# Two float32 attention groups ahead of the MLP, and a pair of token tiles as the MLP's first block

## The chip, the cores and the metric

The kernel runs on one core of a Trainium2 chip. The metric is the device time of one execution in microseconds (us); the trace is of one profiled execution, and its times count from the first instruction. TensorE is called PE, VectorE DVE, ScalarE ACT, GpSimd POOL, and SP is the engine whose queue issues all of this kernel's DMAs. PEld is PE's weight load.

## The reference

Forgetting attention (4 batches, 8 heads, 576 positions, 64 dims), then two MLPs over 2304 tokens:

```python
scores = scale * q @ k.T                      # per head, causal
cum = cumsum(log(clip(f, 1e-4, 1.0)))
scores = where(causal, -1e9, scores + cum[:, None] - cum[None, :])
attn = softmax(scores) @ v
x = attn, heads side by side                  # 2304 x 512
x = leaky(x @ w_in, 0.01) @ w_out             # 512 -> 2048 -> 512
out = leaky(x @ moe2_w_in, alpha) @ moe2_w_out
```

## The kernel before

**Work and tiles.** Tokens are taken in eight *head groups*: each batch is cut into its first 320 positions and its last 256 (`ORDER`: four groups of the first kind, then four of the second). A group of the first kind treats its 8 heads as 4 pairs; a pair has two full units of 128 queries for each head (against 128 and 256 keys) and one packed unit, in which both heads' 64 last queries share 128 rows (against 320 keys). The first MLP goes over token tiles of 256. A *block* is one tile or, where `PAIRS` names it, a pair of tiles; before, the blocks are tiles 0, 1 and 2 alone and the pairs (3,4), (5,6), (7,8). In a block of one tile each matmul streams 256 columns, in a pair 512. Per block there are 16 slices `f` of the hidden dimension, each with 12 matmuls for the hidden values (`moe_h`, L588) and 12 for the output (`moe1_y`, L641). The second MLP follows on its own (L752, L821).

**Number formats.** Most operands are split into a high and a low part in a reduced float32 form (fp32r), with three products. The first `NAT = 16` heads, groups 0 and 1, are computed in plain float32 instead ("native"): each score or value matmul is then two instructions. Before, q and k of a native head stand twice, on partitions 0 to 63 and 64 to 127, and the scale is halved for it (`-SCALE / 2`).

**Weights.** They arrive as float64 bit patterns. Each of the 32 halves of the first MLP's weights is loaded (`raw`, 512 KB), put together by one ACT and three DVE operations (`assemble`, L477, L484, L487, L492) and split into high and low (L395, L400). 18 of the halves are written to `wscr` and loaded again for each later block; 14 stay in SBUF. All this is due in the first block, since that block uses every half once.

**Order.** Nothing is ordered by hand. `Plan.run` plays the program through with a duration for each operation (`t_mm`, `t_act`, ...) and a due time, and what it takes first on a free engine is issued first; every engine and SP's queue then run in that fixed order. `PROL` and `FIRST0` say when the first block is due to begin and how long it lasts.

**Start.** `fg` is loaded, its logarithm summed by a scan (`cum`), and two rows per head are stored to `cum_d` and loaded again for each head, spread over partitions (`cb`, L908). For head 0 alone PE does that spreading (L932). A unit is then: scores (L1095) with a mask matmul (L1100), the decay and the row maximum on DVE (L1109), `exp` on ACT (L1120), 1e-9 and a reciprocal on DVE (L966, L969), the scaling (L1135 or L1137), transposes on PE (L1150), their eviction (`pt`), the value matmuls (L988 native, L998 else) and the split into the MLP's input (`xp`). Group 0 is meant for the prologue; group 1 is planned into block 0, group 2 into block 1, and so on: a block needs the groups that hold its tokens.

**Leaky in the first MLP.** `small` takes 0.01 h from PSUM to `gr` (ACT, L598, or DVE, L600), `leaky1` takes the maximum of both on DVE (L603); then `gr` is split into `g` (hi, lo).

Of the kernel before, what the change touches and what calls it, by code (L numbers as in the profile page):

```python
# [19 lines left out]
P = 128  # L20
# [3 lines left out]
SUBD = 1  # L24
MARGIN = 450
# [11 lines left out]
NY = 2  # L37
TAGS = ("bx bx bx b1 b1 b0 b0", "by by by by bx bx bx", "b0 b0 b1 b1 by by by")
# [14 lines left out]
PAIRS = (3, 5, 7)  # L53
SHIFT = 1
PROL = 26500
FIRST0 = 54400
# [204 lines left out]
def t_mm(n, passes=1):  # L261
    return passes * max(n / 2.4 + 2.5, 109)
# [43 lines left out]
def tile_forgetting_attention_two_moe(ctx: ExitStack, tc, qk0, qk1, v0, v1, fg, w1, w2, alphaT, out):  # L306
# [18 lines left out]
    STREAM = [HALVES[1 + i * (len(HALVES) - 4) // (NSTREAM - 1)] for i in range(NSTREAM)]  # L325
# [61 lines left out]
    pools, rings, att_rings = {"sb": sb, "conv": conv}, {}, []  # L387
# [16 lines left out]
    def ring(tag, bufs, shape, dtype=F32, pool="sb", after=None):  # L404
        def make(slot):
            name = f"{tag}_{slot}"
            return pools[pool].tile(shape, dtype, tag=name, name=name, bufs=1)

        rings[tag] = Ring(bufs, make, after)
        if pool == "att":  # L410
            att_rings.append(rings[tag])
# [15 lines left out]
    xp = [sb.tile([P, 2, NC, 2 * T], F32R, name=f"xp{i}") for i in range(2)]  # L427
    for i in range(4):
        rings[f"x{i}"] = Ring(1, lambda slot, i=i: xp[i // 2][:, :, :, i % 2 * T :][:, :, :, :T])
# [15 lines left out]
    ring("tri", 1, [P, 2 * P], F32R, pool="att")  # L445
# [69 lines left out]
    def weight1(f, half, d):  # L515
        v = assemble(0, f, half, d)
# [53 lines left out]
    def moe_h(bi, f0, hp=None):  # L570
# [5 lines left out]
        xs = [x_tile(k) for k in BLOCKS[bi]]  # L576

# [6 lines left out]
        def mm(i, w, c0, c1):  # L584
            def fn():
                for c in range(c0, c1):
                    for k, (a, s) in enumerate(((0, 0), (0, 1), (1, 0))):
                        pe.matmul(  # L588
                            h()[:, i] if single else h(), lhsT=w.ap[:, a, c * P : (c + 1) * P],
                            rhs=xs[0].ap[:, s, c] if single else xp[(BLOCKS[bi][0] + SHIFT) % 4 // 2][:, s, c],  # L590
# [5 lines left out]
        def small(e):  # L596
            if e == "act":
                act.activation(out=r(), in_=h(), func=AF.Copy, scale=0.01)  # L598
            else:
                dve.tensor_scalar(out=r(), in0=h(), scalar1=0.01, scalar2=None, op0=ALU.mult)  # L600

        def leaky1():
            dve.tensor_tensor(out=r(), in0=h(), in1=r(), op=ALU.max)  # L603
# [16 lines left out]
        plan.op(t_cast(n, True), u, small, r=[hp], w=[gr])  # L620
        on("dve", t_dve(n), u, leaky1, r=[hp], w=[gr])
# [50 lines left out]
    def moe2_x(bi):  # L672
# [3 lines left out]
        for k, tag in enumerate(tags):  # L676
            if tag in ("b0", "b1"):
# [5 lines left out]
                views.append(lambda i=i, at=at: xp[i].rearrange("p a b c -> p (a b c)")[:, at : at + 4 * N2].rearrange(  # L683
# [177 lines left out]
    def attention_heads(gi, hs, d, span):  # L861
# [6 lines left out]
        pt, nm, pair = new("pt"), new("nm"), None  # L868
# [22 lines left out]
        for e, h in enumerate(hs):  # L891
            r, dh = b * H + h, d + each * e
            even = h % 2 == 0
            qk, cb = new("qk"), new("cb")
# [4 lines left out]
            if even:  # L899
                vr = x_raw["v"] = new("vr")  # L900
                on("dma", t_dma(3 * nkt * D * 4 * P), dh - 12e3, lambda: sp.dma_start(
                    out=vr.ap[:, :nkt], in_=g["v"][b, h // 2]), w=[vr])

            def load_qk(qk=qk, h=h):
                sp.dma_start(out=qk.ap[:, : n + keys], in_=g["qk"][b, h])
# [20 lines left out]
            on("dma", t_dma((n + keys) * 4 * P), dh - 7e3, load_qk, w=[qk])  # L926
            if gi == 0 and h < NBC:
# [3 lines left out]
                def broadcast(r=r, bp=bp, m=m):  # L931
                    pe.matmul(  # L932
                        bp.ap[:, :m], lhsT=f32(tri_b.ap[: B * H, r : r + 1]).to_broadcast([B * H, P]),
                        rhs=origin_b[0].ap[: B * H, :m], start=True, stop=True,
# [3 lines left out]
                plan.op(t_cast(m, True), -6e3, lambda en, cb=cb, bp=bp, m=m: cast(en, cb.ap[:, :m], bp.ap[:, :m]), r=[bp], w=[(cb, 0)])  # L938
            else:
                on("dma", t_dma(m * 4 * P), dh - 6.5e3, lambda r=r, cb=cb, m=m: load_cum(lambda: cb.ap[:, :m], r, m), r=[cum_b], w=[(cb, 0)])  # L940
            if pack:
# [3 lines left out]
                on("dma", t_dma(keys * 4 * D), dh - 6e3, lambda r=r, half=half: load_cum(  # L945
                    lambda: pair.ap[half, S - keys :], r, keys), r=[cum_b], w=[(pair, 1 + e)])
            if not native:
                plan.op(t_cast(n + keys), dh - 2e3, qk_hi, r=[qk], w=[k1], shared=True)
# [4 lines left out]
            q, ks = (qk, [qk]) if native else (k1, [k2, k1])  # L953
            for u in full:
                i = len(todo)
                du = d + span * i / count
                todo.append((i, u, attention_scores(g, u, i, du, [(q, ks)], cb, 0, nm, native), [e], du))
            work.append((h, q, ks, v2, o2, even, lo, hi))
        if pack:
            i, u = len(todo), g["units"][-1]  # L960
            du = d + span * i / count
            todo.append((i, u, attention_scores(g, u, i, du, [w[1:3] for w in work], pair, S - keys, nm, native), [0, 1], du))
        for i, u, t, es, du in todo:

            def guard(i=i):
                dve.tensor_scalar(out=nm.ap[:, 3, i : i + 1], in0=nm.ap[:, 2, i : i + 1], scalar1=1e-9, scalar2=None, op0=ALU.add)  # L966

            def recip(i=i):
                dve.reciprocal(out=nm.ap[:, 3, i : i + 1], in_=nm.ap[:, 3, i : i + 1])  # L969

            on("dve", 70, du, guard, w=[(nm, i)])
            on("dve", 75, du, recip, w=[(nm, i)])
            attention_weights(g, u, i, du, t, es, nm, pt, pt_pair if len(es) > 1 else pt_ap, native)
        for e, (h, _, _, v2, o2, even, lo, hi) in enumerate(work):
# [78 lines left out]
    def attention_scores(g, unit, u, d, heads, cb, cb0, nm, native):  # L1053
# [4 lines left out]
        t, dm = new("t"), None if native or pack else new("dm")  # L1058
# [17 lines left out]
        else:  # L1076
            on("pool", t_pool1(nk - split) - 100, d - 1e3, mask, r=[cb], w=[dm])
# [3 lines left out]
        for i, (lo, hi, dec, d0) in enumerate(parts):  # L1081
            if sp_ is None or nk > 512:
                s0, s1 = (0, nk) if nk <= 512 else (lo, hi)
                sp_ = new("a")
                for e, (q, ks) in enumerate(heads):

                    def scores(sp_=sp_, s0=s0, s1=s1, e=e, q=q, ks=ks):
# [280 lines left out]
```

## Time and profile before

| | |
|---|---|
| time, median of 3 runs (lowest, highest) | 1003.78 us (1002.88, 1005.05) |
| profiled execution, first to last instruction | 1001.4 us |
| PE busy | 976.0 us (97%) |
| DVE, ACT, POOL busy | 789.9, 545.3, 94.1 us |
| granted TensorE clock, mean | 0.995 |
| DMA moved | 213.5 MB |

The profiled execution's span and the median of the timed runs differ by 2.4 us; what lies around the span is in that difference. PE's matmuls are pipelined, and the end of one is modelled: a matmul's "mean ns" holds its latency, so the cost of one in a dense stretch is read from the distance between starts.

### The profile page before, as it was taken

Reading aid. Unit: us, or ns where it says so; the run is one execution under the profiler, and the core shown is the slowest. Engines: PE = TensorE matmul, PEld = TensorE weight load, DVE = VectorE, ACT = ScalarE, POOL = GpSimd, SP = SyncE. Lnnn points to the kernel's source line nnn. Section 1 sums busy time; section 2 is a strip of 40 time slices with the busy share of each in tenths; the row PEclk is TensorE's granted clock in tenths of the full one; section 3 lists DMA queues with packets and bytes.
Section 4 is the critical chain, followed back from the end, with each engine's and each line's share of the span. In section 5 each row is a group of like instructions: output and inputs, shape, how many; then the busy total and the mean of one; then the engine's idle time right before and its main releaser. Section 6 shows DMA issues by size and latency. Waiting matters only on the chain.

```text
span 1001.4 us, 16762 instructions
## 1 busy us (share of the span) xinstructions
PE 976.0 (97%) x5538; PEld 866.5 (87%) x5538; DVE 789.9 (79%) x2024; ACT 545.3 (54%) x1239; POOL 94.1 (9%) x169
## 2 busy tenths in 40 slices
PE   5999899999999999999999999999999999999998
PEld 3788799999988888888888888989898898988987
DVE  7889977889999998998788768965686656856563
ACT  6877777788887887887765436311242112321112
POOL 1100111122122212221110000000000000000000
PEclk9999999999999999999999999999999999999999
DMA  8999987788887867987288764543364433544311
GB/s 267 302 316 344 337 268 253 243 293 280 298 299 234 270 214 237 307 275 233 80 288 328 266 209 137 192 143 104 120 206 143 142 103 122 181 136 140 103 52 64
DMA packets 80199, 213.51 MB, mean 213 GB/s; under 512 B 8720, under 2 KB 25520, under 8 KB 80112
## 3 DMA queue, kind: packets, MB, share of 16 engines
q1 hardware_dynamic: 80112, 212.44, 64.0%
q8 instruction: 44, 0.72, 0.3%
q14 instruction: 43, 0.35, 0.1%
HBM read 178.73 MB, written 33.67 MB: 212 GB/s over the span
## 4 chain that ended last, share of the span: by engine, by line
PE 83%; DVE 6%; issue 4%; DMA 4%; ACT 2%; POOL 0%; SPq 0%; ACTq 0%; POOLq 0%; DVEq 0%
PE bank L821 20%; PE bank L752 18%; PE bank L641 16%; PE bank L588 15%; PE bank L1095 5%; PE bank L998 4%; PE bank L1150 4%; DMA w2in<-wa 1%; PE bank L988 1%; DMA vr<-v 1%; DVE pt L1166 1%; DMA raw<-w 1%; DVE t L1109 1%; DMA cb<-cum_d 1%; DVE g L400 0%
## 5 line engine op out<-in xcount | busy, mean ns | idle before, releaser
L821 PE MATMUL bank<-w,g 128*128 128x512 f32 x756 | 196.9, 393 | 0.0
L395 ACT ACTIVATE g<-r 128x384 fp32r<-128x384 f32 x96 | 50.4, 525 | 253.5 <-DVE r L784 232.0
L761 DVE TENSOR_TENSOR r<-bank,r 128x384 f32<-128x384 f32 x168 | 91.1, 554 | 89.8 <-PE bank L752 89.4
L821 PEld LDWEIGHTS bank<-w,g 128*128 128x128 f32 x756 | 140.1, 188 | 21.2
L641 PE MATMUL bank<-g,ws 128*128 128x256 f32 (+1 forms) x720 | 145.5, 343 | 0.3 <-ACT g L395 0.2
L641 PEld LDWEIGHTS bank<-g,ws 128*128 128x128 f32 x720 | 113.3, 191 | 14.0 <-ACT g L395 1.2
L588 PE MATMUL bank<-xp,w 128*128 128x256 f32 (+1 forms) x576 | 115.4, 341 | 0.4 <-ACT pt L395 0.4
L588 PE MATMUL bank<-xp,ws 128*128 128x256 f32 (+1 forms) x576 | 115.4, 341 | 0.0
L588 PEld LDWEIGHTS bank<-xp,w 128*128 128x128 f32 x576 | 90.2, 189 | 12.5 <-ACT pt L395 0.6
L588 PEld LDWEIGHTS bank<-xp,ws 128*128 128x128 f32 x576 | 89.8, 190 | 10.1 <-issue 0.5
L1120 ACT ACTIVATE t<-t,nm 128x128 f32<-128x128 f32 (+4 forms) x144 | 83.4, 580 | 16.3 <-DVE nm L1109 15.4
L641 PE MATMUL bank<-g,w 128*128 128x256 f32 (+1 forms) x432 | 87.9, 342 | 0.0
L1135 ACT ACTIVATE t<-t,nm 128x128 f32<-128x128 f32 (+4 forms) x123 | 70.8, 583 | 21.1 <-DVE nm L969 18.1
L1150 PE MATMUL bank<-tri,t 128*128 128x128 f32 x432 | 72.3, 279 | 7.8 <-DVE gr L603 3.1
L395 ACT ACTIVATE pt<-bank 128x512 fp32r<-128x512 f32 (+6 forms) x174 | 70.0, 425 | 14.8 <-PE bank L1150 13.8
L641 PEld LDWEIGHTS bank<-g,w 128*128 128x128 f32 x432 | 66.9, 190 | 7.8 <-ACT xp L395 0.5
L400 DVE TENSOR_TENSOR g<-r,g 128x384 fp32r<-128x384 f32 x96 | 53.1, 554 | 26.0 <-ACT g L395 25.8
L1061 POOL TENSOR_SCALAR_AFFINE_SELECT dm<-cb 128x448 f32<-128x448 f32 (+1 forms) x96 | 50.1, 524 | 227.3 <-DVE nm L1109 186.8
L1166 DVE TENSOR_TENSOR pt<-bank,pt 128x128 fp32r<-128x128 f32 (+2 forms) x136 | 65.5, 503 | 4.9 <-ACT pt L395 4.1
L1150 PEld LDWEIGHTS bank<-tri,t 128*128 128x128 f32 x432 | 50.8, 142 | 17.7 <-ACT t L1135 5.6
L603 DVE TENSOR_TENSOR gr<-bank,gr 128x512 f32<-128x512 f32 x72 | 49.3, 685 | 13.5 <-ACT gr L598 12.7
L998 PEld LDWEIGHTS bank<-pt,v 128*128 128x128 f32 x416 | 54.9, 188 | 5.1 <-DVE pt L1166 1.1
(138 smaller groups left out, 1753.9 us busy)
## 6 DMA issues: line engine op xcount, KB each, us to landing
ws<-wscr SPq DMA_DIRECT2D x90, 512.0 KB, 4.9
raw<-w SPq DMA_DIRECT2D x64, 512.0 KB, 5.7
wa<-w2in SPq DMA_DIRECT2D x33, 512.0 KB, 3.5
ws<-w2in SPq DMA_DIRECT2D x33, 512.0 KB, 3.4
qk<-qk SPq DMA_DIRECT2D x32, 416.0 KB, 4.4
qk<-qk SPq DMA_DIRECT2D x32, 320.0 KB, 5.0
wscr<-ws SPq DMA_DIRECT2D x18, 512.0 KB, 5.5
cb<-cum_d SPq DMA_DIRECT2D x32, 288.0 KB, 4.4
```

The costliest lines, as they stand in the source:

```text
L395: act.activation(out=out, in_=in_, func=AF.Copy)
L400: (dve if e == "dve" else gps).tensor_tensor(out=out, in0=in0, in1=in1, op=ALU.subtract)
L588: pe.matmul(h()[:, i] if single else h(), lhsT=w.ap[:, a, c * P : (c + 1) * P], rhs=xs[0].ap[:, s, c] if single else xp[(BLOCKS[bi][0] + S ...
L641: pe.matmul(out(c), lhsT=w.ap[:, a, col : col + P], rhs=g.ap[:, s, at : at + n], start=f == 0 and (a, s) == (0, 0) and (c % 2 == 0 or not ...
L752: pe.matmul(b.ap[:, :N2], lhsT=t.ap[:, a, o + c * P : o + (c + 1) * P], rhs=view(k)[:, s, c], start=c == 0 and i == 0, stop=c == 1 and i == 2,
L761: on("dve", t_dve(N2), d + k * step - URGENT, lambda: dve.tensor_tensor(out=out.ap, in0=b.ap[:, :N2], in1=x.ap, op=ALU.add), r=[b] if x is ...
L821: pe.matmul(acc[j * (N2 // P) + t].ap, lhsT=g.ap[:, s, t * P : (t + 1) * P], rhs=w.ap[:, a], start=p == 0 and i == j and (a, s) == (0, 0), ...
L998: pe.matmul(po.ap[:, q:n], lhsT=v2.ap[:, o2 + j, :], rhs=pt_ap(s, e, j, j + 1, q, n), start=s == 0 and j == 0, stop=s == 1 and j == nkt - 1,)
L1120: act.activation(out=t.ap[:, :nk], in_=t.ap[:, :nk], func=AF.Exp, scale=-1.0, bias=nm.ap[:, last, u : u + 1], accum_out=nm.ap[:, 2, u : u ...
L1135: act.activation(out=t.ap[:, :nk], in_=t.ap[:, :nk], func=AF.Copy, scale=nm.ap[:, 3, u : u + 1])
L1150: pe.transpose(tp.ap[:, (j - j0) * P : (j - j0 + 1) * P], t.ap[:, k0 : k0 + P], f32(tri_b.ap[:, :P]))
L1166: dve.tensor_tensor(out=lo, in0=src, in1=f32(hi), op=ALU.subtract)
```

## The change

1. `PAIRS` gets a 0: tiles 0 and 1 become one block, so the blocks are (0,1), 2, (3,4), (5,6), (7,8). `xp` is laid out tile by tile, so a pair's right-hand operand is two runs of 256 columns instead of one of 512.
2. Groups 0 and 1, the native ones, are both planned ahead of the first block, in a pool of their own (`att0`) with deeper rings: 12 score tiles, 3 `qk0`, 3 `cb0`, 3 `vr0`, 2 `pt0`, 4 `nm0`. When all their operations are done, the pool is closed and `att` opened in its place; no operation of a later group starts before. The due times become `PROL = 52000`, `FIRST0 = 99000`.
3. A native head's q and k are loaded once, to 64 partitions: the even head to 0..63, the odd head to 64..127 of one tile. The score matmuls contract over 64 rows, and the scale is whole.
4. The leaky function of the first MLP becomes one ACT operation, `AF.Prelu` with `alpha=0.01`, from PSUM.
5. 1e-9 and the reciprocal are taken for two units at once (`RECIPS = 2`).
6. The planner prices matmuls at `n / 2.4 + 13` ns.
7. The loads of `cum_d` wait for their own group kind's store, not for both; the first 8 weight halves (`FREE`) stay in SBUF and the 18 that are streamed come after them; weight loads from the second slice on wait for the stores of `cum`. The tiles of the prologue's scan lie in the MLP's rings, `tri` in the main pool.

```diff
+RECIPS = 2
...
+NQ0 = 3
+NV0 = 3
+NB0 = 3
+NT0 = 12
...
-PAIRS = (3, 5, 7)
+PAIRS = (0, 3, 5, 7)
...
-PROL = 26500
-FIRST0 = 54400
+PROL = 52000
+PROL0 = 26000
+FIRST0 = 99000
+FREE = 8
...
-    return passes * max(n / 2.4 + 2.5, 109)
+    return passes * max(n / 2.4 + 13, 113)
...
-    STREAM = [HALVES[1 + i * (len(HALVES) - 4) // (NSTREAM - 1)] for i in range(NSTREAM)]
+    STREAM = [HALVES[FREE + i * (len(HALVES) - 3 - FREE) // (NSTREAM - 1)] for i in range(NSTREAM)]
...
-    xp = [sb.tile([P, 2, NC, 2 * T], F32R, name=f"xp{i}") for i in range(2)]
+    xp = sb.tile([P, 4, 2, NC, T], F32R, name="xp")
...
+    ring("qk0", NQ0, [P, 640], pool="att0")
+    ring("vr0", NV0, [P, 3, 3, D], pool="att0")
+    ring("cb0", NB0, [P, 832], pool="att0")
+    ring("t0", NT0, [P, 320], pool="att0")
+    ring("nm0", 4, [P, 4, 5], pool="att0")
+    ring("pt0", 2, [P, 1408], pool="att0")
...
-                            rhs=xs[0].ap[:, s, c] if single else xp[(BLOCKS[bi][0] + SHIFT) % 4 // 2][:, s, c],
+                            rhs=xs[0].ap[:, s, c] if single else xp[:, x0 : x0 + 2, s, c],
...
-        def leaky1():
-            dve.tensor_tensor(out=r(), in0=h(), in1=r(), op=ALU.max)
+        def leaky():
+            act.activation(out=r(), in_=h(), func=AF.Prelu, alpha=0.01)
...
-        plan.op(t_cast(n, True), u, small, r=[hp], w=[gr])
-        on("dve", t_dve(n), u, leaky1, r=[hp], w=[gr])
+        on("act", t_act(n) - 40, u, leaky, r=[hp], w=[gr])
...
-                sp.dma_start(out=qk.ap[:, : n + keys], in_=g["qk"][b, h])
+            def load_qk(qk=qk, h=h, rows=rows):
+                sp.dma_start(out=qk.ap[rows, : n + keys], in_=g["qk"][b, h, : rows.stop - rows.start])
...
-                                sp_.ap[:m, : s1 - s0], lhsT=q.ap[:, qe - m : qe], rhs=k.ap[:, o : o + s1 - s0], start=j == 0,
+                                sp_.ap[:m, : s1 - s0], lhsT=q.ap[rows, qe - m : qe], rhs=k.ap[rows, o : o + s1 - s0], start=j == 0,
...
-                    scale=-SCALE / 2 if native else -SCALE,
+                    scale=-SCALE,
...
+            if i % RECIPS == 0:
+                i1 = min(i + RECIPS, len(todo))
...
-    attention(0, 0.0, PROLOGUE)
+    attention(0, 0.0, PROL0)
+    attention(1, PROL0, PROLOGUE - PROL0)
+    natives = [o for o in plan.ops if any(b.ring in att_rings["att0"] for b in o.bufs)]
+    opened = on(None, 0, 0.0, reopen(nctx, "att", "left", actx), after=natives)
+    for k in att_rings["att"]:
+        k.after = opened
...
-            weight1(f, half, due(0, f) - W1LEAD + 1e3 * half)
-    sent = 1
+            weight1(f, half, due(0, f) - W1LEAD + 1e3 * half, stored if f else [])
+    sent = 2
```

## Rows read from the trace of the kernel before

**Rows 1.** Stretches: length, busy PE, PEld, DVE, ACT, POOL (count), clock, DMA share, GB/s.

```profile
0.00:18.00 18.00, 11.10 (x29) 7.19 (x29) 11.28 (x29) 10.50 (x23) 1.75 (x12) 1.00 0.79 263
18.00:28.30 10.30, 6.43 (x20) 4.58 (x21) 9.10 (x41) 8.25 (x26) 2.13 (x6) 0.67 0.87 275
28.30:75.00 46.70, 44.32 (x295) 37.74 (x294) 38.26 (x136) 36.67 (x113) 4.36 (x8) 1.00 0.94 312
75.00:125.00 50.00, 43.17 (x301) 38.73 (x300) 48.74 (x127) 37.83 (x90) 4.50 (x7) 0.97 0.96 341
...
135.10:201.40 66.30, 66.30 (x557) 66.24 (x556) 54.05 (x196) 51.18 (x147) 11.34 (x29) 1.00 0.77 249
...
300.00:450.00 150.00, 148.86 (x837) 126.94 (x837) 142.24 (x386) 122.55 (x261) 33.99 (x49) 1.00 0.80 257
...
0.00:201.40 201.40, 181.25 (x1271) 163.82 (x1272) 168.76 (x550) 152.82 (x418) 25.74 (x65) 0.97 0.87 291
```

**Rows 2.** SP's queue in order of time: the stores that end blocks 0 and 1.

```profile
135.09 0.90 SPq L662 DMA_DIRECT2D yd<-ysb  x2
...
201.42 0.89 SPq L662 DMA_DIRECT2D yd<-ysb  x2
```

**Rows 3.** The chain that ended last, 0 to 130 us: start, length, what.

```profile
13.82 5.36 DMA cb<-cum_d
...
36.82 6.32 DMA raw<-w
```

**Rows 4.** Line L487 alone, once per weight half: DVE busy, clock, DMA share, GB/s.

```profile
62.00:135.10 73.10, 14.34 (x21) 0.98 0.95 327
```

**Rows 5.** PE in order of time: start, length, line; the bracket is the idle before.

```profile
21.87 0.77 PE L1095 MATMUL bank<-qk 128*128 128x128 f32 x2 [4.16 <-DVE nm L1109]
...
27.96 2.43 PE L988 MATMUL bank<-pt,vr 128*128 128x320 f32 x12
30.23 1.47 PE L1150 MATMUL bank<-tri,t 128*128 128x128 f32 x9
31.54 0.60 PE L1095 MATMUL bank<-qk 128*128 128x256 f32 x2
...
32.03 0.44 PE L1095 MATMUL bank<-qk 128*128 128x128 f32 x2
...
32.36 0.65 PE L1095 MATMUL bank<-qk 128*128 128x256 f32 x2
...
32.91 2.33 PE L988 MATMUL bank<-pt,vr 128*128 128x320 f32 x12
35.08 0.60 PE L1150 MATMUL bank<-tri,t 128*128 128x128 f32 x4
35.61 0.75 PE L1095 MATMUL bank<-qk 128*64 128x320 f32 x2
36.30 0.97 PE L588 MATMUL bank<-xp,w 128*128 128x256 f32 x6
...
51.85 2.38 PE L988 MATMUL bank<-pt,vr 128*128 128x320 f32 x12
```

**Rows 6.** The chain again, dense stretches of a single block and of a pair.

```profile
62.44 1.43 PE bank L588 x12
...
542.61 2.72 PE bank L588 x12
```

**Rows 7.** Groups by line and form: count, busy us, mean ns, idle before.

```profile
L598 ACT ACTIVATE gr<-bank 128x512 f32<-128x512 f32 x68 | 40.4, 594 | 33.4 <-PE bank L588 32.5
...
L1239 ACT ACT_TABLE_LOAD x1 | 1.3, 1283 | 0.0
...
L603 DVE TENSOR_TENSOR gr<-bank,gr 128x512 f32<-128x512 f32 x72 | 49.3, 685 | 13.5 <-ACT gr L598 12.7
...
L969 DVE RECIPROCAL nm<-nm 128x1 f32<-128x1 f32 x144 | 22.1, 158 | 1.4
...
L600 DVE TENSOR_SCALAR gr<-bank 128x512 f32<-128x512 f32 x4 | 2.7, 684 | 0.2 <-PE bank L588 0.2
```

## What the change was predicted to do

> **What bounds the kernel now.** I read the stretches first. From 135 us to 626 us PE is busy practically without a gap, of which one stretch stands for all: 66.30 of 66.30 us between 135.10 and 201.40, at full clock, with DVE at 54 and ACT at 51 [rows 1]. There the kernel is bound by PE, and only fewer or cheaper matmuls help. Before 125 us it is not: PE has gaps in each of the four stretches, and between 75 and 125 us DVE is busy 48.74 of 50 us [rows 1]. So the question is what the first blocks cost beyond their PE work. The second view, SP's queue, gives their ends: block 0 ends at 135.1 us, block 1 at 201.4 us [rows 2]. The third, PE in order of time, prices the work in dense stretches by the distance between starts. A native pair: nine transposes 30.23 to 31.54 = 1.31 us; a unit of 256 keys with its mask 31.54 to 32.03 = 0.49; one of 128 keys 32.03 to 32.36 = 0.33; one half of the packed unit 35.61 to 36.30 = 0.69; the value matmuls 32.91 to 35.08 = 2.17 [rows 5]. Together 1.31 + 2 x (0.49 + 0.33) + 2 x 0.69 + 2.17 = 6.50 us, for the 8 pairs 52.0 us. Twelve matmuls of 256 columns take 1.43 us, of 512 columns 2.72 us, that is 119.2 and 226.7 ns each [rows 6].
>
> So up to 201.4 us PE had 52.0 us of native work, 2 x 384 matmuls x 119.2 ns = 91.5 us of MLP, and 66.3 - 45.8 = 20.5 us of other attention (what block 1's stretch holds beside its 384 matmuls). The sum is 164.0 us; 37.4 us were lost. The fourth view, the chain, says to what. First the start: it passes through a load of `cb` at 13.82 for 5.36 us [rows 3], PE resumes at 21.87 [rows 5], and the clock is 0.67 between 18 and 28.3 us [rows 1]. Then the weights: at 36.82 the chain goes through a load of `raw` of 6.32 us [rows 3], and 21 of the 32 halves are put together only between 62 and 135 us [rows 4], while block 0 has a mere 45.8 us of matmuls to cover that work. That is where DVE is full and PE waits.
>
> **The change, part by part.** *Both native groups first.* PE has no MLP work to fill with until the second group is through, so the end of the native part, T, is the main term. The start is not changed in kind: `cb` of all heads but one still comes through `cum_d`. That its loads wait for one store rather than two saves at most what lies between two issues; I count nothing. PE resumes at 21.9 us. By then it can have done the first pair's scores (6.50 - 1.31 - 2.17 = 3.0 us) and, of head 0 and the next pair, some 1.1 us more: 4.1 us, an estimate; 47.9 us remain. The clock of 0.67 over 10.3 us is 6.8 us at 1.2 instead of 2.4 GHz, in which PE was busy 6.43 us [rows 1]: half of it, 3.2 us, is lost again. For gaps I take what the stretch from 28.3 to 75 us shows, 46.70 - 44.32 = 2.4 us [rows 1]; bounds are nothing and the slow pace among the rivals. T = 21.9 + 47.9 + 3.2 + 2.4 = 75.4 us.
>
> *The pair as first block.* 384 matmuls of 226.7 ns are 87.0 us instead of 91.5, a gain of 4.5 us. Its first matmuls wait for the last eviction and split, an estimate of 1.0 us from the ACT and DVE operations of [rows 7], which are larger. The other attention again takes 20.5 us. The same work is then done at 75.4 + 1.0 + 87.0 + 20.5 = 183.9 us instead of 201.4: 17.5 us gained.
>
> This holds if DVE and ACT keep up. To 201.4 us they were busy 168.8 and 152.8 us [rows 1]. Of DVE's share 16 x 0.685 = 11.0 us of L603 go, and by the reciprocals taken in pairs 24 of 60 units' two small operations, 24 x 2 x 0.158 = 7.6 us (the addition taken at the reciprocal's price) [rows 7]. That leaves 150.2 us in 183.9, 82%, and ACT 83%. The 32 halves now have from the start to the end of an 87 us block rather than of a 46 us one. So PE sets the pace in the pair, and I count nothing for their wait; if the halves came late again, it would cost part of what was lost between 75 and 125 us, 6.8 us of idle PE [rows 1].
>
> *q and k once.* The same number of loads, half the bytes, the same columns in PE: nothing. It is hidden by the native work itself; its price if the clock or the pace suffers stands under the rivals. *Two runs of 256 columns* in the pair's operand: not below nothing, since the columns stay; not over the price of a second matmul start, 2 x 119.2 - 226.7 = 11.7 ns for 4 x 192 = 768 matmuls, 9.0 us. What a matmul costs beyond its columns is about the same at 256 and at 512 (119.2 - 106.7 = 12.5 and 226.7 - 213.3 = 13.4 ns), so it goes by the instruction; I take nothing.
>
> *Leaky on ACT.* 68 of the 72 first steps were on ACT already (594 ns); the second step, 72 x 685 ns = 49.3 us of DVE [rows 7], goes. Where PE is full that buys nothing. Between 300 and 450 us DVE is busy 142.24 of 150 us and PE idles 1.14 us [rows 1]; I take 0.9 of it. ACT needs 594 ns for this shape and DVE 684 [rows 7]. The Trainium skill (ScalarE: Activation LUTs, Rules for kernel authors) advises the opposite for functions like relu and max, VectorE rather than ScalarE; for this float32 tile in PSUM the two rows disagree with it, and by the rule the 0.9 us would be lost, the sum 986.3 us.
>
> *Reciprocals in pairs* make a unit wait for the exponential of its neighbour, with DVE's queue behind it. Twelve score tiles cover that in the native part, the MLP's matmuls later. Without the cover it is one ACT operation, about 0.6 us [rows 7], for each of 24 native batches, 14 us: the slow pace below. *The pool* that opens only after the native part delays the third group's loads to T; 87 us of MLP matmuls cover them. *The planner's price of a matmul* (12 ns more) changes orders; I count nothing and leave it in the range.
>
> The sum: 17.5 + 0.9 = 18.4 us. The profiled span of 1001.4 becomes 983.0 us; the median of the runs lies 2.4 us above the span, so the prediction is 985.4 us.
>
> **The rivals.** *A slow native part* (chance 0.17). PE is alone with chains of scores, DVE, ACT, transposes and evictions, and has nothing to fill gaps. Before, the first group's value matmuls came at 27.96 to 51.85 us, three steps of 7.96 us [rows 5] instead of 6.50, though a weight load and some MLP work were in it. At that pace T is 27.96 + 7 x 7.96 + 2.2 = 85.9 us, 10.5 us later: 995.9 us.
>
> *The clock, the other side* (0.09). The native scores now use 64 of the array's rows, and a stretch of nothing but native work could be held at 1.2 GHz. For it: between 18 and 28.3 us, scores, masks and transposes alone kept PE busy 6.43 us, and the clock stood low for 6.8 us. Against it: from 28.3 to 75 us, mostly native work, it was full [rows 1]. All of it at the low level gives T = 21.9 + 95.8 + 2.4 = 120.1 us and a time of 1030 us. It decides from (18.4 - 2.0) x 2, about 33 us at 1.2 GHz: less than that is still a gain.
>
> *The split operand costs its 11.7 ns* (0.07): 994.4 us.
>
> *Two heads side by side* (0.05). The packed unit's two halves now lie on different rows of the array; if they ran at once, 8 x 0.69 = 5.5 us would go, and the time would be 979.9 us. Masks stand between the other scores. No row shows it, since all of before use 128 rows. The Trainium skill (TensorE: Matmul & The Clock Gate, Part 3) says that matmuls on distinct row groups run concurrently.
>
> *A table load around each Prelu* (0.02). A load takes 1.283 us [rows 7]; two for each of the 56 Prelus that stand among exponentials put 62 us on ACT in the first three tiles and some 54 between 300 and 450 us; against 184 and 150 us that is 30 + 26 us too much, 1041 us. Against it: copies and exponentials already alternate with two loads in all.
>
> *Given back later* (0.04): another order costs PE idle time after 200 us, 15 us or more; 1000 us or over.
>
> **The numbers.** The forecast has 0.56. I take 985.4 us. Without gaps and with halves side by side it is 985.4 - 2.4 - 5.5 - 1.0, some 976 us; the slow pace with the split operand gives 1004.9. The range 974 to 1003 leaves out the clock, the tables and the worst of the slow pace, and holds 0.8. A measurement of this kernel can tell about 0.2%, 2.0 us. Faster: 0.56 + 0.14 (most of the slow pace) + 0.06 + 0.05 + 0.01 = 0.82; same 0.04; slower 0.14.
>
> **What would show it.** The last native value matmul at about 75 us (86: slow pace); the clock full from about 28 us on; the first pair's `yd` stores near 184 us, perhaps later if part of the third group's followers stand before them; PE idle under 3 us between T and there; twelve matmuls of a pair still 2.72 us; two table loads; DVE about 69 us less busy over the span (49.3 + 64 x 0.3); the stretch after the pair as dense as before. Wrong it would be if PE idled in the pair for weights, or if T passed 92 us.

## The result, and the profile after

The change makes the kernel slower: 1011.12 us, median of 4 runs (1010.46 to 1012.45), against 1003.33 us (1000.92 to 1005.05) for the kernel before on the same chip, a ratio of 1.0081 [1.0068, 1.0094]. The prediction said 985.4 us and a range of 974 to 1003: wrong in sign and outside the range. The profiled execution of after spans 1010.7 us, against 983.0 in the sum.

The stretches of after, in the columns of [rows 1]:

```profile
0.00:18.00 18.00, 12.19 (x26) 6.54 (x27) 7.36 (x20) 8.30 (x18) 2.40 (x12) 1.00 0.75 206
18.00:28.30 10.30, 10.17 (x24) 5.42 (x23) 5.79 (x27) 4.22 (x14) 2.18 (x7) 1.00 0.62 184
28.30:75.00 46.70, 46.60 (x203) 31.41 (x203) 28.22 (x120) 35.34 (x126) 6.70 (x13) 1.00 0.66 175
75.00:125.00 50.00, 50.00 (x243) 41.17 (x243) 41.23 (x108) 36.50 (x93) 8.09 (x15) 0.97 0.78 259
300.00:450.00 150.00, 149.08 (x831) 126.50 (x832) 136.49 (x359) 118.43 (x254) 29.83 (x42) 1.00 0.79 265
0.00:201.60 201.60, 193.31 (x883) 146.06 (x883) 150.42 (x450) 143.79 (x397) 38.71 (x76) 0.99 0.74 226
```

PE's gaps are gone as forecast (50.00 of 50 us busy between 75 and 125 us, where before had 43.17), DVE is no longer full there, and DVE's busy time to 201.6 us is 150.42 us (150.2 forecast). And yet nothing is won. The second row shows why to distrust busy time: PE is busy 10.17 of 10.30 us with only 24 matmul instructions.

SP's queue in order of time, after and then before; a block's first `yd` store marks its end:

```profile
201.62 7.14 SPq L670 DMA_DIRECT2D yd<-ysb  x4
...
278.87 0.90 SPq L670 DMA_DIRECT2D yd<-ysb  x2
```

```profile
275.40 0.90 SPq L662 DMA_DIRECT2D yd<-ysb  x2
414.28 0.81 SPq L662 DMA_DIRECT2D yd<-ysb  x2
```

The three first tiles are done at 278.87 instead of 275.40 us. The forecast had them 17.5 us earlier, at 257.9: 21.0 us are missing there. Over the whole span 1010.7 - 983.0 = 27.7 us are missing, so the other 6.7 lie behind that store (the end is 9.3 us later than before's, the store 3.5).

PE of after in order of time (start, length, line; L1113 is the scores, L1118 the mask, L1168 the transposes, L1006 the value matmuls):

```profile
35.13 4.53 PE L1006 MATMUL bank<-pt,vr 128*128 128x320 f32 x12
39.45 1.54 PE L1168 MATMUL bank<-tri,t 128*128 128x128 f32 x9
40.92 0.70 PE L1113 MATMUL bank<-qk 64*128 64x256 f32 x2
41.55 0.33 PE L1118 MATMUL bank<-tri 128*128 128x128 f32 x1
41.81 0.48 PE L1113 MATMUL bank<-qk 64*128 64x128 f32 x2
...
46.17 0.75 PE L1113 MATMUL bank<-qk 64*64 64x320 f32 x2
46.85 0.55 PE L1168 MATMUL bank<-tri,t 128*128 128x128 f32 x3
...
48.00 1.24 PE L1113 MATMUL bank<-qk 64*128 64x320 f32 x4
49.16 0.33 PE L1118 MATMUL bank<-tri 128*128 128x128 f32 x1
...
60.41 0.48 PE L1113 MATMUL bank<-qk 64*128 64x128 f32 x2
...
61.08 0.70 PE L1113 MATMUL bank<-qk 64*128 64x256 f32 x2
...
87.74 2.28 PE L1006 MATMUL bank<-pt,vr 128*128 128x320 f32 x12
```

Three things are to be seen. **The clock.** The twelve value matmuls of a pair take 4.53 us at 35.13 and 2.28 us at 87.74: the first ones ran at half the clock. The clock column reads 1.00 for those stretches, as it also does for before's first 18 us in [rows 1], but equal matmuls at twice the time settle it: PE is at 1.2 GHz until about 40 us, where before's clock was full from 28.3 us [rows 1]. Two more stretches of that time and, in the last row, a second fall that the column does show (length, busy PE, clock, DMA):

```profile
28.30:35.10 6.80, 6.80 (x16) 1.00 0.23 58
35.10:40.20 5.10, 5.10 (x17) 1.00 0.12 33
...
77.80:81.20 3.40, 3.40 (x11) 0.50 0.48 154
```

**The units.** A unit of 256 keys with its mask takes 41.81 - 40.92 = 0.89 us at full clock, where it took 0.49 [rows 5]; one of 128 keys 61.08 - 60.41 = 0.67 for 0.33. The half of a packed unit is unchanged, 46.85 - 46.17 = 0.68 for 0.69. **The end of the native part** is that of the last value matmul, 87.74 + 2.28 = 90.0 us; T was forecast at 75.4.

### The profile page after: what moved, and what is told of

It reads as the page before. It is cut to its first block, busy times and chain, and to the rows that moved or that the text cites. A ratio compares the mean times of both kernels' runs of the same rounds, so it can differ in the third digit from the quotient of the medians.

```text
span 1010.7 us, 15679 instructions
## 1 busy us (share of the span) xinstructions
PE 994.9 (98%) x5154; PEld 850.0 (84%) x5154; DVE 750.2 (74%) x1851; ACT 530.1 (52%) x1216; POOL 93.5 (9%) x164
## 4 chain that ended last, share of the span: by engine, by line
PE 65%; DVE 4%; ACT 1%; issue 1%; ACTq 0%; DVEq 0%
PE bank L829 20%; PE bank L760 17%; PE bank L649 11%; PE bank L603 11%; PE bank L1016 2%; PE bank L1113 2%; PE bank L1168 2%; DVE pt L1184 1%; DVE g L408 0%; DVE t L1127 0%; DVE k L408 0%; DVE r L769 0%; DVE xr L1060 0%; ACT t L1153 0%; ACT pt L403 0%
## 5 line engine op out<-in xcount | busy, mean ns | idle before, releaser
L649 PE MATMUL bank<-g,ws 128*128 128x512 f32 (+1 forms) x540 | 128.6, 374 | 0.0
L603 PE MATMUL bank<-xp,ws 128*128 128x512 f32 (+1 forms) x540 | 125.3, 372 | 0.0
L649 PEld LDWEIGHTS bank<-g,ws 128*128 128x128 f32 x540 | 92.5, 189 | 15.3 <-ACT g L403 0.8
L649 PE MATMUL bank<-g,w 128*128 128x512 f32 (+1 forms) x420 | 101.6, 375 | 0.3 <-ACT g L403 0.3
L603 PE MATMUL bank<-xp,w 128*128 128x512 f32 (+1 forms) x420 | 99.7, 377 | 0.0
L1138 ACT ACTIVATE t<-t,nm 128x128 f32<-128x128 f32 (+4 forms) x144 | 83.5, 581 | 22.0 <-DVE nm L1127 21.7
L603 PEld LDWEIGHTS bank<-xp,w 128*128 128x128 f32 x420 | 73.1, 191 | 12.2 <-DVE nm L1127 0.2
L1184 DVE TENSOR_TENSOR pt<-bank,pt 128x128 fp32r<-128x128 f32 (+2 forms) x136 | 64.0, 503 | 11.7 <-ACT pt L403 10.8
L1153 ACT ACTIVATE t<-t,nm 128x448 f32<-128x448 f32 (+3 forms) x107 | 55.1, 545 | 30.9 <-DVE nm L986 28.0
L1168 PE MATMUL bank<-tri,t 128*128 128x128 f32 x432 | 65.8, 282 | 1.4 <-ACT t L1153 1.1
L408 DVE TENSOR_TENSOR g<-gr,g 128x512 fp32r<-128x512 f32 x72 | 49.8, 691 | 23.2 <-ACT g L403 23.0
L1168 PEld LDWEIGHTS bank<-tri,t 128*128 128x128 f32 x432 | 50.5, 144 | 13.8 <-ACT t L1153 4.1
```

The source lines that it names most:

```text
L408: (dve if e == "dve" else gps).tensor_tensor(out=out, in0=in0, in1=in1, op=ALU.subtract)
L603: pe.matmul(h()[:, i] if single else h(), lhsT=w.ap[:, a, c * P : (c + 1) * P], rhs=xs[0].ap[:, s, c] if single else xp[:, x0 : x0 + 2, s, c],
L649: pe.matmul(out(c), lhsT=w.ap[:, a, col : col + P], rhs=g.ap[:, s, at : at + n], start=f == 0 and (a, s) == (0, 0) and (c % 2 == 0 or not ...
L1138: act.activation(out=t.ap[:, :nk], in_=t.ap[:, :nk], func=AF.Exp, scale=-1.0, bias=nm.ap[:, last, u : u + 1], accum_out=nm.ap[:, 2, u : u ...
L1168: pe.transpose(tp.ap[:, (j - j0) * P : (j - j0 + 1) * P], t.ap[:, k0 : k0 + P], f32(tri_b.ap[:, :P]))
L1184: dve.tensor_tensor(out=lo, in0=src, in1=f32(hi), op=ALU.subtract)
```

## The experiments

Times are medians, ratios against the kernel before on the same chip. "Twice" is the kernel that most others start from.

**twice**: after, with q and k of a native head on 128 partitions and the halved scale, as before had them.

```diff
-NQ0 = 3
+NQ0 = 6
...
-                rows, own, both = slice(e * D, e * D + D), e * 256, 512
+                qk, rows, own, both = new("qk0"), slice(0, P), e * 256, 512
...
-                    scale=-SCALE,
+                    scale=-SCALE / 2 if native else -SCALE,
```

> The changed kernel with q and k of a native head loaded to 128 partitions again, twice over, and the scale halved for it (six q/k tiles). Theory A (the 64-row score matmuls did it, by cost and by clock): a masked unit of 256 keys is 0.49 us from start to start again instead of 0.89, one of 128 keys 0.33 instead of 0.67; the clock is full from about 28 us instead of 40; the native part ends near 75 us instead of 90, and the time falls by 13 to 17 us to about 996. Theory B (a native part without MLP work to fill it is slow whatever the rows): units as before, but the native part ends after 86 us all the same, and the time stays within 4 us of 1011.

Measured: 992.41 us, 0.9897 [0.9882, 0.9912]: 18.7 us less than after, and faster than both kernels. PE in order of time, then two stretches (PE, PEld, DVE, ACT, POOL, clock, DMA) and SP's stores:

```profile
22.07 0.60 PE L1113 MATMUL bank<-qk 128*128 128x256 f32 x2
...
22.56 0.44 PE L1113 MATMUL bank<-qk 128*128 128x128 f32 x2
...
22.89 0.65 PE L1113 MATMUL bank<-qk 128*128 128x256 f32 x2
23.19 0.41 PE L1118 MATMUL bank<-tri 128*128 128x128 f32 x1
23.44 2.33 PE L1006 MATMUL bank<-pt,vr 128*128 128x320 f32 x12
...
36.99 1.18 PE L1113 MATMUL bank<-qk 128*128 128x320 f32 x4
37.82 0.41 PE L1118 MATMUL bank<-tri 128*128 128x128 f32 x1
...
66.14 2.38 PE L1006 MATMUL bank<-pt,vr 128*128 128x320 f32 x12
```

```profile
18.00:28.30 10.30, 10.30 (x55) 7.42 (x54) 8.94 (x44) 10.07 (x40) 2.48 (x7) 0.88 0.85 263
75.00:184.00 109.00, 107.37 (x560) 89.09 (x560) 96.19 (x251) 82.29 (x204) 26.23 (x45) 1.00 0.81 268
258.66:403.32 144.66, 143.26 (x790) 120.42 (x788) 130.59 (x340) 114.50 (x244) 28.39 (x40) 1.00 0.79 263
```

```profile
181.66 7.13 SPq L670 DMA_DIRECT2D yd<-ysb  x4
258.66 0.90 SPq L670 DMA_DIRECT2D yd<-ysb  x2
403.32 0.81 SPq L670 DMA_DIRECT2D yd<-ysb  x2
```

The units are back at 0.49 and 0.33, the value matmuls run at full pace already at 23.44 us, and the native part ends at 66.14 + 2.38 = 68.5 us, 21.5 us earlier than in after. The pair's four stores stand from 181.66 to 188.79 us; the forecast was 183.9.

**once in before**: the kernel before, with q and k of its native heads on partitions 0 to 63 only.

```diff
-                sp.dma_start(out=qk.ap[:, : n + keys], in_=g["qk"][b, h])
+                sp.dma_start(out=qk.ap[: D if native else P, : n + keys], in_=g["qk"][b, h, : D if native else P])
...
-                                sp_.ap[:m, : s1 - s0], lhsT=q.ap[:, qe - m : qe], rhs=k.ap[:, o : o + s1 - s0], start=j == 0,
+                                sp_.ap[:m, : s1 - s0], lhsT=q.ap[: D if native else P, qe - m : qe], rhs=k.ap[: D if native else P, o : o + s1 - s0], start=j == 0,
```

> The kernel before with that part alone: a native head's q and k once, on partitions 0 to 63, scores over 64 rows, whole scale. Theory A: masked units cost 0.89 and 0.67 us there too, and the clock rises later than 28 us; up to 8 x 1.48 = 12 us of PE work more, part of it in gaps that exist anyway: slower by 5 to 15 us, 1008 to 1018. Theory B: no difference beyond 2 us, or a little faster for the smaller loads.

Measured: 1023.54 us, 1.0206 [1.0189, 1.0223], 20.8 us slower. The step has its price without any other part of the change, and with both heads on the same rows, so it doesn't come from the two heads lying on different rows of the array. PE in order of time, then one stretch (busy PE, clock, DMA):

```profile
40.56 0.70 PE L1095 MATMUL bank<-qk 64*128 64x256 f32 x2
41.18 0.33 PE L1100 MATMUL bank<-tri 128*128 128x128 f32 x1
41.44 1.16 PE L1095 MATMUL bank<-qk 64*64 64x320 f32 x4
```

```profile
60.00:78.00 18.00, 17.86 (x90) 0.81 0.48 154
```

Again 41.44 - 40.56 = 0.88 for the unit of 256 keys, and a clock of 0.81 where before had it full.

**half of q zero**: after, with k of both heads in one tile and each head's q on its own 64 partitions, the other 64 set to zero by POOL; the score matmul goes over 128 rows. The products with zeros add nothing, so the scale is whole, and k is loaded once.

```diff
+                gps.memset(qk.ap[D - e * D : P - e * D, :n], 0.0)
...
+                        sp.dma_start(out=kk.ap[j * D : j * D + D, :keys], in_=g["qk"][b, h + j, :D, n : n + keys])
...
-            head = (q, ks, rows, [(qk, e)] if native else [q] + ks)
+            head = (q, ks, slice(0, P), [q] + ks)
```

> The changed kernel with q and k loaded once, as the change has it, but k of both heads in one tile and each head's q on its own 64 partitions of a tile whose other half is set to zero on POOL: the score matmuls run over 128 rows again, half of them zeros, with the whole scale. If what counts is the rows that a matmul addresses, for its cost and for the clock, this is as fast as q and k loaded twice: masked units 0.49 and 0.33 us, full clock by 21 us, 990 to 995. If the clock goes by data that is not zero, the units are short but the clock stays low until about 40 us as with 64 rows, 998 to 1004. If the doubled data itself mattered, 1011.

Measured: 999.46 us, 0.9973 [0.9962, 0.9984], 11.7 us less than after. PE in order of time:

```profile
20.43 0.39 PE L1131 MATMUL bank<-k,q 128*128 128x128 f32 x2
...
20.72 0.65 PE L1131 MATMUL bank<-k,q 128*128 128x256 f32 x2
...
21.27 0.50 PE L1186 MATMUL bank<-tri,t 128*128 128x128 f32 x3
```

The units are short again (0.29 and 0.55 us), at full pace by 20.43 us. So it is the number of rows that the matmul addresses, not the numbers in them, nor the bytes loaded. The time alone would not say so: it lies in the range expected for a low clock, and it is the trace that shows the clock full. Why this version stays 7 us behind "twice" is open. PE idles 10.5 of the first 75 us, 7.8 in "twice", and the pair's first store comes at 187.49 us, 5.8 later.

**One reciprocal at a time** (`RECIPS = 1`), in after and in "twice":

> The changed kernel with one reciprocal per unit again. Theory C (reciprocals in pairs hold back the scaling and thereby PE between 200 and 350 us, where the changed kernel idles 2.9 us of PE and before none): idle there under 1 us and 3 to 6 us faster than the changed kernel, about 1006. Rival: the fewer DVE operations are worth as much, within 2 us of 1011.

> The changed kernel with q and k on 128 partitions and one reciprocal per unit. With 64-row scores this edit cost 9.8 us, but there the clock also fell once more, from about 61 to 78 us, which is 8.5 us by itself. If the clock did it, this run is full from about 20 us on and within 3 us of 992. If the paired reciprocals are worth it by themselves (64 fewer pairs of DVE operations), it is 6 to 10 us slower.

Measured: 1020.88 us, 1.0177 [1.0149, 1.0206], in after, and 994.32 us, 0.9910 [0.9882, 0.9938], in "twice", whose own interval it overlaps. In after the 9.8 us are largely not the reciprocals' own, as the stretch of that run shows (busy PE, clock, DMA):

```profile
60.00:78.00 18.00, 18.00 (x48) 0.53 0.31 71
```

With 64-row scores the clock was at 1.2 GHz for some 17 of these 18 us in this order of the work (0.53 on average); in after it fell for 3.4. Half of the 13.6 us between the two, 6.8 of the 9.8, is the clock's. With 128 rows it didn't fall there, and 1.9 us are left, no more than the intervals allow for nothing. Theory C isn't borne out: one reciprocal per unit is no faster in either kernel.

**A single tile as first block**: "twice" with `PAIRS = (3, 5, 7)` and `FIRST0 = 54400`.

> The changed kernel with q and k on 128 partitions and tile 0 alone as the first block again (FIRST0 = 54400), both native groups still ahead. By the count of matmuls 384 x 11.7 ns = 4.5 us slower; and if the weights' halves then come late as they did before, PE idles in the first block by 5 us or more on top: 1000 or over. Rival: the halves have been put together in the native part, then 995 to 998.

Measured: 1011.46 us, 1.0081 [1.0059, 1.0104]. Both native groups first, without the pair, is slower than before. Busy PE, clock and DMA of the first 125 us:

```profile
0.00:125.00 125.00, 103.57 (x670) 0.99 0.85 301
```

PE idles 21.4 us; in before it idled 125 - 105.0 = 20.0 by the stretches of [rows 1], and in "twice", with the pair, it is busy 117.09 us. Without the pair the kernel is 19.0 us slower, not 4.5: the 32 weight halves want DVE's time (48.14 of 50 us busy between 75 and 125), and one tile's matmuls don't cover that.

**Leaky in two steps again** (ACT or DVE takes 0.01 h, DVE the maximum), in after and in "twice":

```diff
-            act.activation(out=r(), in_=h(), func=AF.Prelu, alpha=0.01)
+                act.activation(out=r(), in_=h(), func=AF.Copy, scale=0.01)
...
+            dve.tensor_tensor(out=r(), in0=h(), in1=r(), op=ALU.max)
```

> The changed kernel with the leaky function in two steps again (0.01 h on ACT or DVE, maximum on DVE). If the single Prelu is worth what was predicted, 1 to 3 us slower than the changed kernel, 1012 to 1014. Rival: Prelu on ACT stands in the way of attention's exponentials and scalings there, and two steps are 2 to 5 us faster.

> The changed kernel with q and k on 128 partitions and the leaky function in two steps again. With 64 rows this edit cost 13.7 us. If that is the leaky function's own worth in this order (16 x 0.685 us of DVE more in the pair, and as much in each later pair, with DVE at 86 to 97% there): 8 to 14 us slower than 992.4. Rival: that was the clock or an accident of the order; then within 3 us.

Measured: 1024.86 us, 1.0217 [1.0200, 1.0235], and 1008.61 us, 1.0058 [1.0043, 1.0073]: 13.7 and 16.2 us, not 0.9. In "twice" with two steps the third tile's first store comes at 269.72 us, 11.1 later than in "twice", so most of the loss lies before it. The block after it, 144.66 us in "twice", takes 418.04 - 269.72 = 148.32. From its second store on PE idles 5.1 us in that block, instead of 1.4:

```profile
269.72 0.39 SPq L677 DMA_DIRECT2D yd<-ysb  x1
...
270.94:418.04 147.10, 141.98 (x777) 117.29 (x776) 134.37 (x345) 111.62 (x240) 29.93 (x43) 1.00 0.77 251
```

Before carried the two steps with 1.1 us of idle PE in 150 [rows 1], under due times of its own. How much of the 13.7 to 16.2 us is the operation, and how much due times that don't suit it, the two runs don't separate.

**The planner's price** (the old `n / 2.4 + 2.5`) in "twice", and the new one alone in the kernel before:

> The changed kernel with q and k on 128 partitions (992.4 us) and the planner's old price of a matmul (n / 2.4 + 2.5 ns). Between 125 and 300 us that kernel idles 4.3 us of PE, before none. Theory P: the truer price takes from the order the slack that PE's lateness against the plan gave the attention chains, so PE meets them unready. Then the old price brings the idle time there under 1.5 us and the time to 984 to 989. Rival Q: the stalls come from what the stage holds (a pair's end, fewer matmuls to choose from, two reciprocals at once): within 2 us of 992, or slower.

> The kernel before with the new price of a matmul alone. Theory P: PE idles between 135 and 450 us (before 1.1 us), by 3 us or more, and the kernel is 3 to 10 us slower, 1006 to 1013. Rival Q: within 2 us of 1003.

Measured: 993.99 us, 0.9906 [0.9887, 0.9926], no difference that can be told; and 1046.42 us, 1.0426 [1.0399, 1.0453], 43 us slower. Two stretches of the latter (busy PE, clock, DMA):

```profile
125.00:300.00 175.00, 162.87 (x1200) 0.97 0.73 230
300.00:450.00 150.00, 139.80 (x756) 0.98 0.73 235
```

Before's PE idled 0.2 us in the first of these. The price changes no instruction; but with due times set for another price the order leaves PE waiting 22 us in these two stretches, far more than the 3 us that theory P asked for. In "twice" theory P fails: the old price brings nothing.

**Less work for DVE**: "twice" without the operation that puts the sign on the first MLP's weights (32 of 0.69 us, 22 us of DVE), so that these signs are missing in the output.

> The changed kernel with q and k on 128 partitions, and the sign operation of assemble left out for the 32 halves of the first MLP's weights (those weights lose their signs): 32 x 0.69 = 22 us less of DVE, all before 184 us, nothing else touched. If DVE (96.2 of 109 us busy between 75 and 184 us) is what holds PE up there, PE's 1.6 us of idle time in that stretch and the stalls after it shrink, and the time falls by 5 to 10 us to 983 to 987. Rival: the stalls are latencies in the chain of one attention unit, which less work on DVE does not shorten: within 2 us of 992.4.

Measured: 987.31 us, 0.9845 [0.9831, 0.9860], 5.1 us less than "twice". The third tile's first store comes 2.4 us earlier, and the block of pair (3,4) is 3.3 us shorter, though no operation was taken out of it:

```profile
256.22:397.58 141.36, 140.31 (x774) 118.75 (x772) 125.43 (x329) 110.84 (x237) 25.84 (x39) 1.00 0.78 262
```

In that block DVE is busy 125.43 us instead of 130.59, and PE has 774 matmuls instead of 790: with less to do before it, the planner places the work anew. Load and order change together in this run.

**Other due times** in "twice": the followers' lead 10 us longer (`LEAD1 = 34000`, `LEAD2 = 64900`), the same with the old price, the native part due later (`PROL = 64000`, `PROL0 = 32000`), and earlier (`PROL = 44000`, `PROL0 = 22000`, from 52000 and 26000; the expectation of that run quotes both starting values wrongly).

> The changed kernel with q and k on 128 partitions (992.4 us) and attention due 10 us earlier against the block that needs it (LEAD1 34000, LEAD2 64900). If PE's 4.3 us of idle time between 125 and 300 us, and the stalls under it, come from attention chains that are planned too late for their block, most of it goes: 985 to 989. Rival: those stretches have DVE at 86 to 97% busy, and what is due earlier pushes out weights or the MLP's own splits: 991 or over.

> The same with the planner's old price of a matmul as well. The old price took the loss out of 200 to 450 us but put PE idle time of some 6 us into 125 to 200 us, where DVE was full with the third group and the last weight halves. If earlier attention thins that out: 982 to 987. Rival: it only moves it, 992 or over.

> The changed kernel with q and k on 128 partitions and the first block due when the native part is really over there: PROL 64000 for 52000, PROL0 32000 for 26000 (its last native value matmul ends at 68.4 us). If the stalls after 125 us come from due times that have run 12 us ahead of the clock, so that the third group's attention is always behind what is due, 3 to 8 us faster: 984 to 989. Rival: only the order between due times counts and all move together: within 2 us.

> Version with q and k on 128 partitions (992.4 us), with the due times of the third group's prologue 10 us earlier (PROL 44000 for 54000, PROL0 22000 for 32000). If the 8 us that this version misses against the forecast come from due times that lag behind the work between 150 and 300 us, it gets faster: 985 to 990 us, with PE's idle time between 125 and 300 us falling from 4.3 us towards 1. If they come from the load on VectorE alone, the order hardly matters: 991 to 996 us, the same idle time. Ten us later cost 4.9 us, so a loss on this side too (994 us or more) means that the due times stand near their best and are not the cause.

Measured: 993.74 us, 0.9912 [0.9897, 0.9927]; 1001.92 us, 0.9998 [0.9989, 1.0008]; 997.31 us, 0.9953 [0.9938, 0.9968]; 993.74 us, 0.9906 [0.9877, 0.9936]. None is better than "twice": no lag of the due times that these four settings touch is the cause of what is missing there.

## Why the prediction was wrong

**The step that failed is "q and k once ... nothing".** It held the columns to be the cost. Two prices came instead, each more than half of the gain forecast for the whole. First, a unit of 64-row scores and a 128-row mask takes 0.40 us (256 keys) or 0.34 us (128 keys) more; 2 x (0.40 + 0.34) = 1.48 us per pair, 11.8 us for eight. The price lies at the change of shape between a score and its 128-row neighbour, not in a 64-row matmul as such. Both traces have places that show it: the first half of a packed unit and a unit of 256 keys, four score matmuls in a row without a mask between them (x4 at 48.00 and at 36.99, named by the form of the first). They take 49.16 - 48.00 = 1.16 us in after and 37.82 - 36.99 = 0.83 in "twice", 0.33 more for both, and the scores of the unit of 256 keys alone pay as much, 41.55 - 40.92 = 0.63 against 23.19 - 22.89 = 0.30. Ahead of the mask's weights (49.16) PEld stands idle for 0.33 us in after; in "twice" (37.79) it doesn't. The second half of a packed unit, which already used other columns of the array than its neighbours (128\*64 weights in [rows 5]), stays the same, 0.68 for 0.69.

Second, the clock: PE is busy at 1.2 GHz for 10.17 us between 18 and 28.3, 6.80 + 5.10 up to 40.2, and 3.40 at 77.8. Half of these 25.5 us is 12.7, where 3.2 were counted. Together 9.5 + 11.8 = 21.3 us beyond the sum (the units that ran at the low clock are in both), against 21.0 us missing at the third tile's store and 21.5 us between the native parts of after and "twice". "Once in before" gives 20.8 us in the other kernel, and "twice" gives 18.7 back.

That 21.3 meets 21.0 so closely is in part luck. T itself is only 90.0 - 75.4 = 14.6 us late, since the sum's T was 6.9 us too long for what "twice" shows; and from T to the third tile's store both kernels need more than the 182.5 us of the sum, 188.9 in after and 190.2 in "twice". Nor do the two native parts end on equal work: after has 21 of the MLP's matmuls before its T, "twice" 15.

**The rival of the clock** had the right sign, mechanism and place, at 0.09, and the wrong argument against it: that the clock was full between 28.3 and 75 us was a statement on 128-row scores. It was priced for all the native work (1030 us) and said to decide from 33 us at 1.2 GHz. It was 25.5 us. By the sum the clock alone would have left a gain; the loss needed the longer units too, which no rival had.

**What held.** With 128 rows the pair's stores begin at 181.66 us (183.9 forecast), though T came earlier than forecast, at 68.5 (75.4): the sum's gaps (2.4 us) and slow clock (3.2) hardly occurred, as PE is busy 46.37 of 46.60 us from 21.9 to 68.5, at full clock. PE's gaps before 125 us went. Nine matmuls with the split operand in a dense stretch of after take 97.67 - 95.63 = 2.04 us, 227 ns each, so the split costs nothing:

```profile
95.63 2.20 PE L603 MATMUL bank<-xp,w 128*128 128x512 f32 x9
97.67 0.61 PE L649 MATMUL bank<-g,w 128*128 128x512 f32 x2
```

There are two table loads as before, so Prelu brings none:

```profile
L1214 ACT ACT_TABLE_LOAD x1 | 1.3, 1283 | 0.7 <-PEq L1378 0.7
...
L1260 ACT ACT_TABLE_LOAD x1 | 1.3, 1283 | 0.0
```

**Terms mis-sized without harm to the sum.** "The pair as first block" was given 4.5 us, and taking it out costs 19.0; "leaky on ACT" was given 0.9, and taking it out costs 13.7 to 16.2 here, due times that don't suit included. Both relieve DVE, and the sum had their effect in "82%, ... So PE sets the pace", where it isn't seen whose it is. The place where the 0.9 us was looked for gave little: between 300 and 450 us PE idles 0.92 us in after, 1.14 in before. DVE's whole busy time fell by 789.9 - 750.2 = 39.7 us, not by 69. In part the planner gave DVE other shared operations in return (37 scalings at L1155 where before had 20, 9.4 us more); the rest wasn't traced. The Trainium skill (ScalarE: Activation LUTs, Rules for kernel authors) advises VectorE for relu and max. The two runs with the maximum on VectorE are 13.7 and 16.2 us slower here, where VectorE is the engine near its bound; no run has the whole function on VectorE in one operation.

**What is missing with 128 rows**, 992.41 - 985.4 = 7.0 us of median and 8.1 of span. Of the 8.1, 0.8 are missing at the third tile's store (258.66 for 257.9), the rest behind it. The 82% was an average. Up to 184 us DVE is busy 55.46 + 96.19 = 151.7 us in "twice" (150.2 forecast), but 96.19 of 109 us, 88%, from 75 us on: only 11 of the 32 halves were put together before, 21 behind. PE idles 1.6 us in that stretch all the same. In the pair (3,4) the chain of waits of "twice" lies on DVE alone, but for short issue times, from 282.53 to 289.09 us (first and last of its 11 longest steps there):

```profile
282.53 0.60 DVE g L408
...
288.40 0.69 DVE pt L1184
```

Taking 22 us from DVE brings 5.1 us back, so DVE's load has a part in it; but the order changed with it, and PE idles no more than 1.40 us in the whole block, 1.11 in the same block of before. At 258.66 us "twice" is 16.7 us ahead of before, at the end 10.3, and 5.8 of the 6.4 us between are lost in this block (144.66 us, 138.88 before). The 16 matmuls more that "twice" has left behind the third tile's store (3687 against 3671) make at most 16 x 0.227 = 3.6 us of the 6.4. How the remaining 2.8 us or more divide between DVE's load and the order stays open: neither the price nor other due times brought them back.

**The rival of two halves at once** wasn't put to the test: after's trace has no two halves of one unit right behind each other. So what the Trainium skill (TensorE: Matmul & The Clock Gate, Part 3) says of distinct row groups is neither shown nor refuted here; a lone half took 0.68 us.

## What to carry to other kernels

A matmul over half the array's rows has the same columns and not the same cost: price it beside its neighbours (0.89 us for 0.49 next to a 128-row mask, once per change of shape) and ask what it does to the clock, above all in a stretch where nothing else runs. An average load of 82% can hide a stretch at 88%: count an off-path engine over the stretch in which it can be used. An order that a planner makes from prices and due times is one setting; a price changed alone (43 us) or an operation put back alone (14 to 16 us) can measure the mismatch as well as the thing.

## What the runs showed of the hardware

PE was busy with hardly a gap (10.17 of 10.30 us, then 6.80 of 6.80) with 64-row scores among 128-row masks, and the clock stayed at 1.2 GHz until about 40 us; with 128 rows of the same numbers, or of zeros in half of them, it was full from about 20 us on. Later in the native part the clock fell again where 64-row scores ran or had just run, for 3.4 us in after and for some 17 us in the version with single reciprocals. Such scores aren't the only occasion: before, without them, has a clock of 0.97 between 75 and 125 us [rows 1], with PE busy 43.17 of 50 us. A busy share of PE and a granted clock are thus two readings, and neither tells the other. Going from 64-row scores to a 128-row matmul cost 0.33 us more than staying at 128 rows, and two score units in a row paid it once.
